# Reordering the opening of a convolution and feed-forward kernel: when the filter is turned, when two output rows are multiplied, and which PSUM tiles they use

## The chip, the cores and the metric

The kernel runs on one core of a Trainium2 chip. The metric is the device time of one execution in microseconds. A core has TensorE (PE for matmuls, PEld for the loading of their weights), VectorE (DVE), ScalarE (ACT), GpSimd (POOL) and SyncE (SP), each with its own queue of instructions that it works off in order. Matrix results are written to PSUM, from which VectorE and ScalarE copy them to SBUF. DMA transfers are issued from queues too, here mostly from SP and POOL.

## The reference

The input is x, 2048 tokens of 576 channels in bfloat16. Two layers of the same form follow each other, with the same weights:

```
x = x + A(layernorm(x))        # A: q * (causal convolution of kv along the tokens + kv * D)
x = x + B(layernorm(x))        # B: (gelu(x Wg) * (x Wu)) Wd, hidden width 4608
```

with, in A,

```
k_shift[t] = sum over j in 0..3 of shift_k[:, 3 - j] * k[t - j]
kv = k_shift * v
y  = irfft(rfft(kv padded) * rfft(ssm_k padded))[:2048] + kv * ssm_D
A  = q * y
```

The long convolution is along the tokens, one filter of 2048 taps for each of the 576 channels. The layer norms have no weights.

## The kernel before

**Blocks.** The tokens are cut into four blocks of 512, the feed-forward part into units of 512 tokens, and within a block a token t = 4q + i belongs to tile i (0 to 3), with q over 128 partitions. The convolution is done in blocks: each block of kv and each block of the filter is transformed by matmuls with tables of cosines and sines (`W`, `Wx`), the spectra are multiplied on VectorE, and the inverse transform is again a set of matmuls that sum up in PSUM. A spectrum has four parts kt of real and imaginary rows; the output has four tiles Y0 to Y3 (`straight(mt, kts)` issues, for output tile mt and each kt in kts, the products of two parts with two halves of 288 columns: four matmuls for each kt).

**The whole.** After an opening of some 38 us, written out by hand in `begin`, the feed-forward matmuls of the first unit begin (`half_gu`, line 1604), and from there to the end a planner (`Pace`, `fill`) lays the convolution of later blocks and all VectorE and ScalarE work between long runs of gate/up (line 1684) and down matmuls (line 1718). The planner works when the program is built, on its own estimates of time; the order it makes is fixed.

**The opening, in order of TensorE's work.** (1) Matmuls on constants fill the time until the first data come. (2) Small matmuls spread the short filter `shift_k` and the vector `ssm_D` over partitions. (3) The first block of k is turned (`L932`), four 128-column blocks minus the rest of the channels: 384 channels go by TensorE, 192 by VectorE (`wx`). (4) The first 512 taps of the filter, loaded as channels by taps in `hn[0]` (four blocks of 128 channels and one of 64, `nd` = 4), are turned by `turn_h(0)` (line 956) into two PSUM tiles, one for tiles i = 0 and 1, the other for 2 and 3, and ScalarE copies them to `hT0` (line 961). Before, POOL adds `ssm_D` to the filter's tap 0 (line 917), which lies in i = 0; `turn_h` therefore takes i in the order 2, 3, 1, 0. (5) `shift_taps` (line 817) convolves k with its four taps: 14 matmuls for the first two channel blocks, 7 for the third; VectorE multiplies them with v (line 977). (6) The transforms of filter and kv alternate (`even`, `odd` at line 227, `kfwd` at line 218). An `even` result is copied by ScalarE (line 990) before `odd` adds to the same PSUM tile; `apart` on VectorE (line 232) makes the two other spectrum parts from the two. `kacc(kt)` multiplies kv and filter spectra on VectorE (lines 358, 360, 361) and `put` writes spectra to DRAM from POOL's queue. (7) `turn_h(1)` turns the filter's second 512 taps. (8) `straight` makes Y0 and Y2, then Y1 and Y3 (line 414).

**The relay to the first feed-forward matmul.** For tiles 0 and 2: `head.gate` on VectorE multiplies with the normalized x and adds (lines 1493, 1496), `mean` and `sq` give mean and sum of squares (VectorE 1502, ScalarE 1219), `std` the root (ScalarE 1513), `norm` the normalized rows with their first 64 columns copied behind them (VectorE 1436, 1437, 1439), `turn` nine transposes on TensorE (line 1458), and `copy` brings them to `xnT` (line 1465) in two pieces of five and four column blocks. `keep_y` copies an output tile from PSUM to SBUF on ScalarE (line 420). Tiles 1 and 3 pass their gates a little later. `head.idle(6)` issues six transposes of a constant. A one-element Gelu (`warm`) makes ScalarE load the Gelu table.

**PSUM.** The pool `psp` (`new`, `new_t`, tag "pr") has three tiles of two banks, `cpsp` (`small`, `small_t`, tag "cps") has one. A tile that is asked for gets the space of one that is no longer needed, and its first matmul waits until the last reader is done. In the old order Y0 and Y2 lie in `psp`, Y1 and Y3 one after the other in the single tile of `cpsp`, and both pieces of a `head.turn` in one tile of `psp`.

**Queues around the change.** SP's queue holds the loads in the order k, filter rows 512 to 575, filter rows 0 to 511, v, x, the forward tables, the second filter block, the inverse tables (line 877), then three pairs of gate/up weights and, after the opening's scratch memory is free, three loads of down weights (line 1183). A load reuses one of a few semaphores and waits for the load that used it before. POOL's queue holds, mixed, small vector steps (the means of `act_sum` and `row_sum` at line 1211, the roots at 1226 and 1227), a rearrangement of `shift_k` that goes through DRAM (`skT`, lines 971, 973, 1048), and DMA issues; it also has a limited number of semaphores to reuse.

Of the kernel before, what the change touches and what calls it, by code (L numbers as in the profile page):

```python
# [22 lines left out]
P = 128  # L23
# [3 lines left out]
RT = BS // P  # L27
# [58 lines left out]
class Conv:  # L86
# [743 lines left out]
    def begin(self, head, tables):  # L830

        tc, nc, D, KS = self.tc, self.nc, self.D, self.KS
        nd = D // P
        width = lambda db: min(P, D - db * P)
        with ExitStack() as es:
# [12 lines left out]
            hn = [tmp.tile([P, nd + 1, BS], BF16, name=f"hn{b}") for b in range(2)]  # L848
            hT0 = tmp.tile([P, RT, D], BF16, name="hT0")
# [6 lines left out]

            def load_h(b):
                cols = slice(b * BS, (b + 1) * BS)
                nc.sync.dma_start(out=hn[b][0:D - nd * P, nd, :], in_=self.hk[nd * P:D, cols])
                nc.sync.dma_start(out=hn[b][:, 0:nd, :], in_=self.hk[0:nd * P, cols].rearrange("(b p) t -> p b t", p=P))  # L860

            nc.vector.memset(full, 1.0)
            nc.vector.memset(ones[:], 1.0)
# [26 lines left out]
            ps = new()  # L890
# [11 lines left out]
            ps = new()  # L902
# [10 lines left out]
            nc.scalar.copy(out=dcol[:, 0:nd], in_=ps[:, 1, at:at + nd])  # L913
            nc.scalar.copy(out=dcol[0:D - nd * P, nd:nd + 1], in_=ps[0:D - nd * P, 1, at + nd:at + nd + 1])
            busy(idle, 4)
            for lo, hi, w in ((nd, nd + 1, D - nd * P), (0, nd, P)):
                nc.gpsimd.tensor_tensor(out=hn[0][0:w, lo:hi, 0], in0=hn[0][0:w, lo:hi, 0], in1=dcol[0:w, lo:hi], op=ALU.add)

            k, v = self.kt_[0], self.vt_[0]
# [5 lines left out]
            DBS = [(0, 1), (2,)]  # L925
            pts = []
            for n, dbs in enumerate(DBS):
                pt = new_t() if n else small_t()
# [18 lines left out]
                tt(out=wx[0][:], in0=wx[0][:], in1=wx[1][:], op=ALU.add)  # L947
            tt(out=v[:, :, rest], in0=wx[0][:], in1=v[:, :, rest], op=ALU.mult)

            def turn_h(b, pt):  # L950

                hv = hn[b][:].rearrange("p b (q i) -> p b i q", i=RT)
                for i in (2, 3, 1, 0):
                    for db in range(nd + 1):
                        w = width(db)
                        nc.tensor.transpose(pt[i // 2][:, i % 2, db * P:db * P + w], hv[0:w, db, i, :], self.ident[0:w, 0:w])  # L956
                return pt

            def copy_h(hT, pt):
                for g in (1, 0):  # L960
                    nc.scalar.copy(out=hT[:, 2 * g:2 * g + 2, :], in_=pt[g][:, :, 0:D])
            copy_h(hT0, turn_h(0, (new_t(), new_t())))
            out = []
            for n, dbs in enumerate(DBS):
                o = (new() if n else small())[:].rearrange("p e (i c) -> p e i c", i=RT)
                for e, db in enumerate(dbs):
                    self.shift_taps(k, kT, dg, P, db, o[:, e])
                out.append(o)
            head.act_sum(3)
            for j in range(KS):  # L970
                nc.gpsimd.tensor_copy(out=self.skc[0:1, j, :], in_=sk1[:, :, j])
# [47 lines left out]
            def straight(mt, kts, first=False, last=False, parts=(0, 1)):  # L1019

                terms = []
                for kt in kts:
                    for part in parts:
                        if mt % 2 == 0:
                            s, minus = part, mt == 2 and kt % 2 == 1
                        elif kt % 2 == 0:
                            s, minus = part, kt == 2
                        else:
                            s, minus = 1 - part, ((mt == 1) == (part == 1)) != (kt == 3)
                        w = Wn[:, mt // 2, :] if minus and (mt, s) in ((1, 1), (3, 0)) else self.inv_w(mt, s, minus)  # L1030
                        terms.append((w, A[(part, kt)]))
                self.inverse(0, mt, terms, Y[mt], first, last)
# [47 lines left out]
            head.act_sq(1)  # L1080
            head.act_sq(3)
            head.gate(0, Y[0])
# [20 lines left out]
            nc.scalar.activation(out=warm[:], in_=head.zero, func=ACT.Gelu_apprx_tanh)  # L1103
# [705 lines left out]
```

## Time and profile before

| | us |
|---|---|
| median of 3 runs | 913.95 |
| the three runs | 914.36, 912.22, 913.95 |
| profiled execution | 912.26 |
| its span, first to last instruction | 910.4 |
| TensorE busy in the span | 904.5 |
| VectorE, ScalarE, POOL busy | 575.9, 331.6, 158.8 |
| first gate/up stream begins (line 1604) | 37.95 |

The profiled execution's time is longer than its span by 1.9 us, which lie around the instructions. A row of the timeline has start and length in microseconds from the span's start, the engine, the line of the kernel, the operation, output <- input by their names in the program with their sizes, and how many instructions the row joins; a bracket gives the engine's idle time before the first of them and what ended it. The start of the next row of an engine, rather than the end of the last, tells TensorE's pace, since its matmuls overlap. A row of a stage table has the stage's length, then busy time and count for PE, PEld, DVE, ACT and POOL, the granted clock, the DMA share and GB/s. Lines are those of the kernel before; in the changed kernel they move by up to 6.

### The profile page before, as it was taken

How to read it: one execution, taken by the hardware profiler on the slowest of the kernel's cores; microseconds unless marked ns; L12 is line 12 of the kernel's file. 1: busy time of each engine (PE TensorE's matmuls, PEld its weight loads, DVE VectorE, ACT ScalarE, POOL GpSimd, SP SyncE). 2: the span in 40 equal slices, each digit the busy share in tenths (PEclk: the TensorE clock that was granted, in tenths of full speed). 3: DMA queues.
4: the chain of work that ended last, by engine and by line, in shares of the span. 5: the costliest groups of instructions: out<-in, count | busy, mean ns of one | idle time of the engine just before them, and what ended most of it. 6: DMA issues, size and time to landing. Idle time of an engine off the chain costs nothing.

```text
span 910.4 us, 19239 instructions
## 1 busy us (share of the span) xinstructions
PE 904.5 (99%) x8173; PEld 526.6 (58%) x8173; DVE 575.9 (63%) x977; ACT 331.6 (36%) x621; POOL 158.8 (17%) x337
## 2 busy tenths in 40 slices
PE   9999999999999999999999999999999999999998
PEld 6786646556465465564655655646646546556555
DVE  7889986689889885797898855442332335333332
ACT  6765445523323255453124133551121224321211
POOL 3413405120113031420104002320000003100000
PEclk9999999999999999999999999999999999999999
DMA  9999998858519519785925801971620721977620
GB/s 250 351 217 282 238 253 131 208 157 170 183 53 249 123 16 168 211 154 114 268 65 131 181 2 38 170 159 26 132 78 4 154 80 27 170 171 178 135 64 27
DMA packets 129530, 131.73 MB, mean 145 GB/s; under 512 B 43682, under 2 KB 121251, under 8 KB 129444
## 3 DMA queue, kind: packets, MB, share of 16 engines
q1 hardware_dynamic: 119232, 93.47, 49.5%
q0 software_dynamic: 10208, 37.02, 13.0%
q8 instruction: 64, 1.05, 0.5%
q14 instruction: 22, 0.18, 0.1%
q10 hardware_dynamic: 4, 0.01, 0.0%
HBM read 108.35 MB, written 11.80 MB: 132 GB/s over the span
## 4 chain that ended last, share of the span: by engine, by line
PE 99%; ACT 0%; DMA 0%; DVE 0%; issue 0%; ACTq 0%; DVEq 0%
PE gu L1684 59%; PE dn L1718 31%; PE gu L1604 3%; PE cps L281 1%; PE ps L414 1%; PE cps L414 1%; PE ps L281 0%; PE ps L218 0%; PE cps L218 0%; PE ps L227 0%; PE pt L956 0%; DMA dvec<-in_A_ssm_D_dram 0%; PE xps L1458 0%; PE cps L817 0%; PE cpt L956 0%; PE cps L887 0%
## 5 line engine op out<-in xcount | busy, mean ns | idle before, releaser
L1684 PE MATMUL gu<-xnT,wgu 64*128 64x512 bf16 x4968 | 540.7, 376 | 0.0
L1684 PEld LDWEIGHTS <-wgu 64*128 64x128 bf16 x4968 | 239.7, 94 | 294.4 <-issue 5.7
L1693 ACT ACTIVATE ga<-gu 128x512 f32<-128x512 f32 x258 | 153.9, 597 | 450.9 <-PE gu L1684 442.5
L1694 DVE TENSOR_TENSOR hT<-ga,gu 128x512 bf16<-128x512 f32 x258 | 177.0, 686 | 200.7 <-ACT ga L1693 199.1
L1718 PE MATMUL dn<-wd,hT 128*128 128x288 bf16 x2304 | 292.3, 286 | 0.0
L1718 PEld LDWEIGHTS <-hT 128*128 128x128 bf16 x2304 | 223.5, 98 | 65.6 <-issue 9.5
L1754 DVE TENSOR_TENSOR x_c<-x_c,dn 128x576 f32<-128x576 f32 x64 | 48.2, 752 | 57.2 <-PE dn L1718 56.9
L1211 POOL TENSOR_SCALAR nm<-s 128x1 f32<-128x1 f32 x60 | 21.2, 354 | 271.6 <-DVE x_c L1749 210.8
L1219 ACT ACTIVATE junk<-x_c,nm 128x576 bf16<-128x576 f32 x48 | 36.8, 768 | 26.5 <-POOL nm L1211 25.9
L1227 POOL TENSOR_TENSOR rstd<-ve,neghalf_t 128x1 f32<-128x1 f32 x62 | 40.2, 648 | 5.2
L554 POOL DMA_DIRECT2D hr<-Hd x32 | 17.4, 544 | 118.3 <-DVE prod L360 117.3
L1226 POOL TENSOR_SCALAR ve<-ss 128x1 f32<-128x1 f32 x62 | 22.3, 360 | 54.4 <-ACT junk L1219 54.3
L1283 ACT ACTIVATE xn<-x_c,nb,rstd 128x576 bf16<-128x576 f32 (+1 forms) x48 | 28.6, 644 | 5.9 <-POOL nb L1231 5.7
L284 ACT COPY eo<-cps 128x576 f32<-128x576 f32 x31 | 19.9, 641 | 27.9 <-PE cps L281 24.4
L1740 DVE TENSOR_TENSOR ob<-x_c,dn 128x576 bf16<-128x576 f32 x15 | 11.3, 753 | 29.0 <-PE dn L1718 25.7
L1583 ACT ACTIVATE ga<-gu 128x512 bf16<-128x512 f32 x26 | 15.5, 597 | 31.8 <-PE gu L1684 24.9
L1604 PE MATMUL gu<-xnT,wgu 64*128 64x256 bf16 x432 | 24.8, 269 | 0.5 <-ACT xnT L1465 0.3
L1604 PEld LDWEIGHTS <-wgu 64*128 64x128 bf16 x432 | 21.2, 94 | 3.6 <-issue 1.1
L361 DVE TENSOR_TENSOR prod<-prod 128x576 bf16<-128x576 bf16 x48 | 22.0, 458 | 1.7
L429 POOL DMA_DIRECT2D out_dram<-ob x12 | 6.8, 562 | 91.8 <-issue 47.0
L244 DVE SCALAR_TENSOR_TENSOR eo<-eo 128x576 f32<-128x576 f32 x22 | 16.3, 752 | 5.8 <-ACT eo L284 5.8
L1261 DVE SCALAR_TENSOR_TENSOR x_c<-g_t,rstd,x_c 128x576 f32<-128x576 f32 x16 | 13.0, 815 | 8.6 <-POOL rstd L1227 8.6
(166 smaller groups left out, 589.9 us busy)
## 6 DMA issues: line engine op xcount, KB each, us to landing
wgu<-in_B_w_gate_dram SPq DMA_DIRECT2D x45, 576.0 KB, 6.5
wd<-in_B_w_down_dram SPq DMA_DIRECT2D x30, 864.0 KB, 8.3
wgu<-in_B_w_up_dram SPq DMA_DIRECT2D x45, 512.0 KB, 8.0
hr<-Hd POOLq DMA_DIRECT2D x32, 288.0 KB, 5.7
kr<-Kd POOLq DMA_DIRECT2D x24, 288.0 KB, 6.0
Kd<-kc POOLq DMA_DIRECT2D x12, 288.0 KB, 6.5
k<-in_A_k_dram POOLq DMA_DIRECT2D x3, 1008.0 KB, 12.4
wgu<-in_B_w_up_dram SPq DMA_DIRECT2D x45, 64.0 KB, 7.7
```

The source lines that it names most:

```text
L361: nc.vector.tensor_tensor(out=dst, in0=pr[:, 0, :], in1=pr[:, 1, :], op=ALU.subtract if part == 0 else ALU.add)
L1211: nc.gpsimd.tensor_scalar(out=v["nm"][:], in0=v["s"][:], scalar1=-1.0 / D, scalar2=None, op0=ALU.mult)
L1219: nc.scalar.activation(out=junk[:], in_=get_x(), func=ACT.Square, bias=v["nm"][:, 0:1], accum_out=v["ss"][:])
L1226: nc.gpsimd.tensor_scalar(out=ve[:], in0=v["ss"][:], scalar1=1.0 / D, scalar2=EPS, op0=ALU.mult, op1=ALU.add)
L1227: nc.gpsimd.tensor_tensor(out=v["rstd"][:], in0=ve[:], in1=neghalf_t[:, 0:1], op=ALU.pow)
L1283: nc.scalar.activation(out=xn[:, lo:hi], in_=x_c[c][:, j, 0:hi - lo], func=ACT.Identity, scale=v["rstd"][:, 0:1], bias=v["nb"][:, 0:1])
L1604: nc.tensor.matmul(pair[:, s, e * 256:(e + 1) * 256], lhsT=w[r0:r0 + HK, k, gi * P:(gi + 1) * P], rhs=xnT[r0:r0 + HK, blk_of[k], tok], sta ...
L1684: nc.tensor.matmul(pair[:, s, :], lhsT=w[r0:r0 + HK, k, gi * P:(gi + 1) * P], rhs=xnT[r0:r0 + HK, b, :], start=(k == 0), stop=(k == NKC - 1))
L1693: nc.scalar.activation(out=ga[:], in_=pair[:, 0, :], func=ACT.Gelu_apprx_tanh)
L1694: nc.vector.tensor_tensor(out=hT[:, fi, :], in0=ga[:], in1=pair[:, 1, :], op=ALU.mult)
L1718: nc.tensor.matmul(part[h][:, h, 0:HW], lhsT=hT[:, fi, at * P:(at + 1) * P], rhs=wd[2 * wb + fi // WT][:, fi % WT, h * HW:(h + 1) * HW], s ...
L1754: nc.vector.tensor_tensor(out=xh, in0=xh, in1=acc[:, :, 0:HW], op=ALU.add)
```

## The change

All of it lies in `begin`.

1. The filter loads change places (the 512 rows first, then the 64), and so do POOL's two additions of `ssm_D`.
2. `turn_h` takes a list of channel blocks and goes through i in order. For the first filter block the four blocks of 128 channels are turned and copied (two copies of 2 x 512 elements), then the first 14 `shift_taps` matmuls are issued, then the four 64-row turns and two copies of 2 x 64, then the last 7 taps. For the second filter block all 128-row turns come first and then the four 64-row ones; the `cps` tile is turned first, the copies stay as they were.
3. Of Y2's matmuls, those of kt = 0 alone (four) are issued ahead of Y0's last four, instead of those of kt = 0 and 2 (eight).
4. Y3 moves to a tile of `psp`. The six idle transposes go. `keep_y` of Y2 moves ahead, in front of tile 2's square, and that of Y1 behind tile 2's root; Y3's last four matmuls move ahead of tile 2's turn.
5. Tile 2's turn writes its first five blocks to a tile of `psp` and its last four to the one of `cpsp`. The one-element Gelu moves behind tile 2's copy.

The instructions after the opening, and their order on every engine, are the same in both kernels.

```
-                nc.sync.dma_start(out=hn[b][0:D - nd * P, nd, :], in_=self.hk[nd * P:D, cols])
                 nc.sync.dma_start(out=hn[b][:, 0:nd, :], in_=self.hk[0:nd * P, cols].rearrange("(b p) t -> p b t", p=P))
+                nc.sync.dma_start(out=hn[b][0:D - nd * P, nd, :], in_=self.hk[nd * P:D, cols])
...
-            for lo, hi, w in ((nd, nd + 1, D - nd * P), (0, nd, P)):
+            for lo, hi, w in ((0, nd, P), (nd, nd + 1, D - nd * P)):
...
-            def turn_h(b, pt):
+            def turn_h(b, pt, dbs):
                 hv = hn[b][:].rearrange("p b (q i) -> p b i q", i=RT)
-                for i in (2, 3, 1, 0):
-                    for db in range(nd + 1):
+                for i in range(RT):
+                    for db in dbs:
...
-            copy_h(hT0, turn_h(0, (new_t(), new_t())))
-            out = []
-            for n, dbs in enumerate(DBS):
-                o = (new() if n else small())[:].rearrange("p e (i c) -> p e i c", i=RT)
+            def taps_of(dbs, ps):
+                o = ps[:].rearrange("p e (i c) -> p e i c", i=RT)
                 for e, db in enumerate(dbs):
                     self.shift_taps(k, kT, dg, P, db, o[:, e])
-                out.append(o)
+                return o
+            pt, out = (new_t(), new_t()), []
+            turn_h(0, pt, range(nd))
+            copy_h(hT0, pt, slice(0, nd * P))
+            out.append(taps_of(DBS[0], small()))
+            turn_h(0, pt, (nd,))
+            copy_h(hT0, pt, slice(nd * P, D))
+            out.append(taps_of(DBS[1], new()))
...
-            copy_h(self.hT1, turn_h(1, (small_t(), new_t())))
+            pt = small_t(), new_t()
+            for dbs in (range(nd), (nd,)):
+                turn_h(1, pt, dbs)
+            copy_h(self.hT1, pt, slice(0, D), (1, 0))
...
             straight(0, (0, 2, 1), True)
-            straight(2, (0, 2), True)
+            straight(2, (0,), True)
             kacc(3)
             straight(0, (3,), last=True)
-            straight(2, (1, 3), last=True)
+            straight(2, (2, 1, 3), last=True)
...
-            self.keep_y(0, 1, Y[1])
-            head.idle(6)
-            Y[3] = small()
-            straight(3, (0, 2), True)
             head.gate(2, Y[2])
             head.mean(2)
+            self.keep_y(0, 2, Y[2])
+            Y[3] = new()
+            straight(3, (0, 2), True)
             head.sq(2)
             head.std(2)
             head.norm(0)
             head.turn(0)
             self.apart0(A, 0, 0)
-            straight(3, (1,))
+            straight(3, (1, 3), last=True)
+            self.keep_y(0, 1, Y[1])
             head.norm(2)
+            head.copy(0, nc.vector.tensor_copy)
+            head.turn(2, small_t())
+            head.copy(2, nc.scalar.copy, nc.vector.tensor_copy)
             nc.scalar.activation(out=warm[:], in_=head.zero, func=ACT.Gelu_apprx_tanh)
-            head.copy(0, nc.vector.tensor_copy)
-            head.turn(2)
-            straight(3, (3,), last=True)
-            head.copy(2, nc.scalar.copy, nc.vector.tensor_copy)
             self.keep_y(0, 3, Y[3])
-            self.keep_y(0, 2, Y[2])
```

More of the change, by code (lines that the diff above doesn't have):

```diff
@@ L948, in begin, with copy_h @@
             tt(out=v[:, :, rest], in0=wx[0][:], in1=v[:, :, rest], op=ALU.mult)
-            def turn_h(b, pt):
+            def turn_h(b, pt, dbs):
                 hv = hn[b][:].rearrange("p b (q i) -> p b i q", i=RT)
-                for i in (2, 3, 1, 0):
-                    for db in range(nd + 1):
+                for i in range(RT):
+                    for db in dbs:
                         w = width(db)
                         nc.tensor.transpose(pt[i // 2][:, i % 2, db * P:db * P + w], hv[0:w, db, i, :], self.ident[0:w, 0:w])
[L957 to L961, printed above, removed]
-            copy_h(hT0, turn_h(0, (new_t(), new_t())))
-            out = []
-            for n, dbs in enumerate(DBS):
-                o = (new() if n else small())[:].rearrange("p e (i c) -> p e i c", i=RT)
+            def copy_h(hT, pt, cols, order=(0, 1)):
+                for g in order:
+                    nc.scalar.copy(out=hT[:, 2 * g:2 * g + 2, cols], in_=pt[g][:, :, cols])
+            def taps_of(dbs, ps):
+                o = ps[:].rearrange("p e (i c) -> p e i c", i=RT)
                 for e, db in enumerate(dbs):
                     self.shift_taps(k, kT, dg, P, db, o[:, e])
-                out.append(o)
+                return o
[6 more added lines that the diff above has]
+            out.append(taps_of(DBS[1], new()))
             head.act_sum(3)
```

2 lines of the change are left out of this document (1 added, 1 removed).

## The prediction

> **What bounds the kernel now.** I read the page's busy shares, then stages by window, then the opening's timeline engine by engine (columns there: start, length, engine, line, operation, and in brackets the idle time before and what ended it).
>
> ```profile
> PE 904.5 (99%) x8173; PEld 526.6 (58%) x8173; DVE 575.9 (63%) x977; ACT 331.6 (36%) x621; POOL 158.8 (17%) x337
> ```
>
> ```profile
> 7.00:38.00 31.00, 29.56 (x254) 22.35 (x254) 26.44 (x53) 25.57 (x47) 14.55 (x29) 1.00 1.08 304
> 38.00:910.40 872.40, 869.29 (x7880) 500.33 (x7879) 545.87 (x905) 302.85 (x567) 143.10 (x301) 1.00 0.61 138
> ```
>
> From 38 us on TensorE (the column after the length) has no idle time worth a name: 869.29 of 872.40. What the opening gains before its first gate/up matmul therefore reaches the end, and what it loses too. The instruction order after that point is the same in both kernels.
>
> In the opening the page hides the bound: PE is "busy", but for two stretches another engine sets the pace.
>
> ```profile
> 5.69 0.56 DVE L942 TENSOR_TENSOR wx<-k,sx 128x768 bf16<-128x768 bf16 x1 [0.44 <-ACT sx L912]
> 5.84 0.45 POOL L917 TENSOR_TENSOR hn<-hn,dcol 64x1 bf16<-64x1 bf16 x1 [4.55 <-ACT dcol L914]
> 6.00 1.06 PE L932 MATMUL cpt<-ident,k 128*128 128x128 bf16 x8
> 6.86 0.63 PE L932 MATMUL pt<-ident,k 128*128 128x128 bf16 x4
> 7.09 0.55 DVE L946 TENSOR_TENSOR wx<-kx,sx 128x768 bf16<-128x768 bf16 x1
> 7.10 1.01 ACT L937 COPY kT<-cpt 128x1024 bf16<-128x1024 bf16 x1 [0.15 <-PE cpt L932]
> 7.36 2.70 PE L956 MATMUL pt<-ident,hn 128*128 128x128 bf16 x20
> 7.38 0.32 POOL L917 TENSOR_TENSOR hn<-hn,dcol 128x4 bf16<-128x4 bf16 x1 [1.09 <-DMA hn<-in_A_ssm_k_dram]
> 8.01 0.59 ACT L937 COPY kT<-pt 128x512 bf16<-128x512 bf16 x1
> 10.00 1.92 PE L817 MATMUL cps<-dg,kT 128*128 128x512 bf16 x14
> 11.12 0.69 ACT L1204 ACTIVATE junk<-x_b 128x576 bf16<-128x576 bf16 x1
> 11.75 1.03 PE L817 MATMUL ps<-dg,kT 128*128 128x512 bf16 x7
> 12.62 1.14 PE L227 MATMUL ps<-hT,W 128*128 128x288 bf16 x8
> 15.12 0.72 POOL L973 DMA_DIRECT2D skT<-skc  x1 [0.31 <-POOL skc L971]
> ```
>
> ```profile
> 15.36 1.42 DVE L232 SCALAR_TENSOR_TENSOR h<-eo,ps 128x576 bf16<-128x576 f32 x2 [0.93 <-ACT h L995]
> ...
> 28.29 0.46 DVE L361 TENSOR_TENSOR yb<-prod 128x576 bf16<-128x576 bf16 x1
> 30.03 0.81 DVE L1493 SCALAR_TENSOR_TENSOR x_c<-x_b,nm,ps 128x576 f32<-128x576 bf16 x1 [1.29 <-PE ps L414]
> ```
>
> VectorE runs from 15.36 to 28.75 without a recorded wait: its last product (kacc(3)) cannot come earlier unless 15.36 does, and that waits for TensorE's first transform through ScalarE. From 30.03 a relay runs: gate, mean, square, root, norm, turn, copy, first gate/up matmul at 37.95.
>
> **First turns and taps.** Turns are paced by TensorE's rate: eight from 6.00 to 6.86, 0.107 us each; late ones take 0.056 (below: nine from 34.91 to 35.41). The 20 before last 7.36 to 10.00. Afterwards the first turn needs the D-added row, so it waits for POOL's 128x4 add. The large load is issued first now; its landing (about 7.36 before) can move by the small load's share only, a tenth of its bytes, to 7.05 at best. POOL's two L917 adds both ended 0.05 to 0.06 after a VectorE tensor_tensor (5.69+0.56 against 5.84+0.45; 7.09+0.55 against 7.38+0.32), so I take the same end, 7.70, and the first turn at 7.75; the other bound is no wait, 7.28. Sixteen turns of 0.107 bring the taps to 9.5; 14 taps last 1.75 (10.00 to 11.75), to 11.25. The four 64-row turns: in the second tile ten turns last 0.97 (24.83 to 25.80, below), eight of them 0.45, so a lone 64-row turn costs 0.26, mostly the switch of row count before and after. Four together: 0.26+3x0.056=0.43, bounded by 4x0.26=1.04. Taps of the last block, 0.87, end at 12.55 instead of 12.62: **gain 0.07**, between -0.54 and +0.34. Their four copies become two of 1024 and two of 128 elements (1.01 each, and by the slope from 0.59 to 1.01 about 0.28, at most 0.59); they end about 12.3, hidden while the taps run to 12.55, and act_sum (0.69) behind them ends 13.0, before ScalarE's next copy can start, after the transform's first four matmuls (0.123 each, below; 12.55+0.49+0.2=13.2).
>
> [...]
>
> **Second turns, and Y2 behind Y0.**
>
> ```profile
> 24.83 1.04 PE L956 MATMUL pt<-ident,hn 128*128 128x128 bf16 x10
> 25.80 1.07 PE L956 MATMUL cpt<-ident,hn 128*128 128x128 bf16 x10
> 26.80 4.09 PE L414 MATMUL ps<-yb,W 128*128 128x288 bf16 x32
> 30.73 0.90 PE L414 MATMUL cps<-yb,W 128*128 128x288 bf16 x6
> ```
>
> The 20 turns shrink from 1.97 to 16x0.056+0.43=1.33: PE reaches Y0 at 26.09. A product matmul takes 3.93/32=0.123. Twelve of Y0 and four of Y2 end 28.06, two more 28.30; the last pair needs kacc(3), 28.75-0.07=28.68. So Y0's last starts 28.85 instead of 29.63 (26.80+23x0.123), and the gate starts at 29.25 instead of 30.03: 0.78, of it **0.71 new**. PE idles 0.4 there; with eight of Y2 ahead it would be there at 28.5 and lose nothing, so the moved four are worth nothing if the turns shrink, and up to 0.49 if they don't. The turns' first half now waits for kc's copy out of the single cps tile; that copy follows the same matmuls that PE has just left, and is done about 0.1 before PE comes; each 0.1 late would cost nothing either until the 0.4 idle is used up.
>
> **The relay's end.**
>
> ```profile
> 32.80 0.82 DVE L1496 SCALAR_TENSOR_TENSOR x_c<-x_c,rstd,x_b 128x576 f32<-128x576 f32 x1
> 33.25 0.63 ACT L420 ACTIVATE y<-cps 128x576 bf16<-128x576 f32 x1
> 33.94 0.65 PE L414 MATMUL cps<-yb,W 128*128 128x288 bf16 x4 [0.74 <-ACT y L420]
> 34.91 0.67 PE L1458 MATMUL xps<-ident,xn 128*128 128x128 bf16 x9
> 35.19 1.28 ACT L1103 ACT_TABLE_LOAD   x1
> 35.41 0.65 PE L414 MATMUL cps<-yb,W 128*128 128x288 bf16 x4
> 36.02 0.18 DVE L1439 COPY xn<-xn 128x64 bf16<-128x64 bf16 x1
> 36.04 0.68 PE L1458 MATMUL xps<-ident,xn 128*128 128x128 bf16 x9
> 36.11 0.81 DVE L1465 COPY xnT<-xps 128x640 bf16<-128x640 bf16 x2
> 36.75 0.69 ACT L1465 COPY xnT<-xps 128x640 bf16<-128x640 bf16 x1
> 37.35 2.83 SPq L1183 DMA_DIRECT2D wd<-in_B_w_down_dram  x3
> 37.48 0.42 DVE L1465 COPY xnT<-xps 128x512 bf16<-128x512 bf16 x1 [0.55 <-ACT xnT L1465]
> 37.95 5.96 PE L1604 MATMUL gu<-xnT,wgu 64*128 64x256 bf16 x106 [0.17 <-DVE xnT L1465]
> ```
>
> Y3 leaves the single cps tile, so the 0.74 wait on Y1's copy goes, and the six idle matmuls (6x0.056) that lay in it; keep_y(2) takes that copy's place (0.63) before the second square. Norm 2 ends at 36.20-0.78=35.42. PE must not be late: 16 of Y1 and 8 of Y3 end 33.4, turn 0 starts at 33.8 with its norm, eight of Y3 end 35.28, norm 2's rows come at 35.20: level. Its fifth turn waits for the 128x64 copy (35.47), done 35.69; ScalarE's copy 35.73 to 36.42; VectorE, after turn 0's copies (35.33+0.81=36.14), copies the other four blocks from their own tile without the 0.55 wait for ScalarE: 36.1 to 36.52. The stream starts at 36.57 instead of 37.95: **another 0.60**, down to 0 if that wait returns in another form.
>
> Given back: the Gelu table load and its warm-up move behind ScalarE's copy and hold Y3's copy to 36.42+1.28+0.2+0.63=38.5, which tile 3's gate reads. VectorE, after tile 1's gate (two passes of 0.81 and 0.82 from 36.52, with small steps between), would want it at 38.3. If tiles 1 and 3 come 0.2 late to their turns, PE may wait that long: I charge 0.1, between 0 and 0.2. SP's three wd loads wait for that warm-up: 37.9 instead of 37.35; the gate/up matmuls cover them, the first down matmul starting at 64.83-1.38. On SP the inverse twiddles (L877) and the first wgu load behind them now wait for the large hn load instead of the small one:
>
> ```profile
> 64.83 0.42 PE L1718 MATMUL dn<-wd,hT 128*128 128x288 bf16 x2
> ```
>
> these are first read at 26.1 and 36.5, so a slip of a microsecond or two costs nothing.
>
> **Sum.** 0.07+0.71+0.60-0.1=1.3 us. The profiled execution took 912.26 for a span of 910.4; the sum gives 910.95. That execution is quick: the runs took 914.36, 912.22 and 913.95 (median 913.95, mean 913.5), a spread of 2.1 that no row explains. From the mean, 912.2. I forecast the middle, **911.6**. Changes within 0.3% (2.7 us) are about what a measurement of this kernel can't tell from none.
>
> **Rivals.**
> 1. The relay's end pays nothing: 0.60 lost to a new wait (PE late at turn 2, ScalarE's y2 copy late, 0.63, ahead of the square). For it: both meet within 0.1 us. Gain 0.7: 912.2. Chance 0.17.
> 2. Full rate comes late, and it ends slower. The spacing fell from 0.107 to 0.056 near 9.5, inside the turns. The halt before the first turn could delay that. Each us longer costs 0.48; from 2.7 us later (12.2) the gain is gone, and 3.5 later, the length from 6.00 to 9.5, gives 1.7 lost: 913.3, where the kernel before stands at 911.6+1.3=912.9. Against: the halt is 0.4 at most. Chance 0.1.
> 3. POOL's queue slips. act_sum ends 1.1 later, so skT (15.12) leaves later, and with it the POOL DMAs ahead of tile 2's rstd.
>
> ```profile
> 28.35 0.54 POOL L424 DMA_DIRECT2D Hd<-h  x1 [2.44 <-DVE prod L360]
> 29.20 0.56 POOL L1227 TENSOR_TENSOR rstd<-ve,neghalf_t 128x1 f32<-128x1 f32 x1
> ```
>
> The 2.44 wait absorbs 1.1; rstd (29.76) is needed at 32.80-0.78=32.0. From 3.3 late on each us costs one: at 5 late the 1.7 lost give 913.3. Chance 0.05.
> 4. The change does more: the add doesn't wait (0.34) and nothing is given back: 0.34+0.71+0.60=1.65, 911.2. Chance 0.13.
>
> The forecast keeps 0.55. [...]
>
> Range 909.8 to 914.0: the upper gain from the quickest run, less run scatter, to the lost gain from the slower runs. Against 913.95, faster by over 0.3% means under 911.2: a third of the forecast's and half of rival 4's weight and a little of rival 1, 0.31. Slower by over 0.3% needs two of the losses together: 0.07.
>
> **What would show it.** First L956 at 7.3 to 7.8, 16 turns 1.7 long; first L227 near 12.5; VectorE's gate L1499 near 29.3 with PE waiting for DVE yb before Y0's last pair; no ACT y wait before Y3; the gate/up stream at 36.6, VectorE's last xnT copy not waiting for ScalarE. Wrong if the 64-row turns cost 0.26 each in a row, if PE still takes 0.107 per turn or more past 10, or if the stage after 38 shows new PE gaps.

## The result and the profile after

The changed kernel takes 910.68 us (median of ten runs, 909.91 to 911.10), the kernel before 912.65 (ten runs, 911.75 to 915.46): the ratio is 0.9971, with a 95% interval of 0.9961 to 0.9982, that is 1.6 to 3.6 us less. The forecast was 911.6, its range 909.8 to 914.0. The profiled executions took 912.26 before and 910.61 after, their spans 910.4 and 908.8.

First the page's busy shares of the changed kernel, and its two stages by window (columns as before):

```profile
PE 903.0 (99%) x8167; PEld 526.0 (58%) x8167; DVE 575.7 (63%) x977; ACT 331.6 (36%) x623; POOL 157.7 (17%) x337
```

```profile
7.00:38.00 31.00, 29.63 (x278) 23.49 (x278) 27.93 (x55) 26.08 (x49) 13.94 (x28) 1.00 1.08 301
38.00:908.80 870.80, 867.61 (x7852) 498.53 (x7846) 544.07 (x901) 302.35 (x567) 142.53 (x301) 1.00 0.61 139
```

Behind 38 us TensorE idles 3.19 us, 3.11 before: nothing new there, and the 1.60 by which that stretch is shorter was won ahead of it. So the opening has to be read. The timeline of the changed kernel, first turns and taps:

```profile
5.85 0.36 POOL L917 TENSOR_TENSOR hn<-hn,dcol 128x4 bf16<-128x4 bf16 x1 [4.55 <-DMA hn<-in_A_ssm_k_dram]
6.43 0.19 POOL L917 TENSOR_TENSOR hn<-hn,dcol 64x1 bf16<-64x1 bf16 x1 [0.23 <-DMA hn<-in_A_ssm_k_dram]
7.17 1.91 PE L956 MATMUL pt<-ident,hn 128*128 128x128 bf16 x16
8.88 2.24 PE L817 MATMUL cps<-dg,kT 128*128 128x512 bf16 x14
11.05 0.32 PE L956 MATMUL pt<-ident,hn 64*128 64x64 bf16 x4
11.30 1.05 PE L817 MATMUL ps<-dg,kT 128*128 128x512 bf16 x7
12.19 1.14 PE L227 MATMUL ps<-hT,W 128*128 128x288 bf16 x8
14.93 1.42 DVE L232 SCALAR_TENSOR_TENSOR h<-eo,ps 128x576 bf16<-128x576 f32 x2 [1.19 <-ACT h L1000]
```

POOL's add to the large part is done at 6.21, where the prediction had 7.70. The first turn (7.17, 7.36 before) waits for nothing; of these 0.19, 0.08 is the wait for the load that TensorE had before, and 0.11 is chance: the D vector that TensorE spreads at L909 came at 4.25 here and at 4.36 in the profile before. Then the sixteen turns take 1.71 (7.17 to 8.88), and the first transform comes at 12.19: 0.43 earlier than the 12.62 before. VectorE's first sum follows 0.43 earlier too (14.93, 15.36 before). The same view, second turns and first gate:

```profile
24.40 0.61 PE L956 MATMUL cpt<-ident,hn 128*128 128x128 bf16 x8
25.48 0.23 PE L956 MATMUL pt<-ident,hn 64*128 64x64 bf16 x2
25.64 2.38 PE L414 MATMUL ps<-yb,W 128*128 128x288 bf16 x18
28.36 1.88 PE L414 MATMUL ps<-yb,W 128*128 128x288 bf16 x14 [0.34 <-DVE yb L361]
28.88 0.81 DVE L1499 SCALAR_TENSOR_TENSOR x_c<-x_b,nm,ps 128x576 f32<-128x576 bf16 x1 [0.58 <-PE ps L414]
```

The second turns take 1.24 (24.40 to 25.64) instead of 1.97. TensorE has eighteen matmuls done and waits 0.34 for VectorE's last product, as forecast. The gate is at 28.88, 1.15 earlier than before, 0.72 of it new. The relay's end, again in the timeline:

```profile
33.41 0.68 PE L1464 MATMUL xps<-ident,xn 128*128 128x128 bf16 x9 [0.24 <-DVE xn L1443]
35.39 0.69 ACT L1471 COPY xnT<-xps 128x640 bf16<-128x640 bf16 x1 [0.67 <-PE xps L1464]
35.69 0.41 DVE L1471 COPY xnT<-cpt 128x512 bf16<-128x512 bf16 x1
36.09 1.28 ACT L1114 ACT_TABLE_LOAD   x1
36.13 4.11 PE L1610 MATMUL gu<-xnT,wgu 64*128 64x256 bf16 x72 [0.56 <-DVE xnT L1471]
37.50 0.63 ACT L420 ACTIVATE y<-ps 128x576 bf16<-128x576 f32 x1
38.16 0.82 DVE L1499 SCALAR_TENSOR_TENSOR x_c<-x_b,nm,y 128x576 f32<-128x576 bf16 x1 [0.22 <-ACT y L420]
```

(The Gelu table load is line 1103 before and 1114 here, since it moved.) The two last copies run side by side (35.39 to 36.08 and 35.69 to 36.10). Before, the first two gate/up matmuls had run at 37.49 and the third at 37.95; now the third starts at 36.24, 0.11 behind the first. From the gate to the third the relay took 7.92 (30.03 to 37.95) and takes 7.36 (28.88 to 36.24): 0.56 less. With it the stream is 1.71 earlier, and the span 1.66 shorter (910.41 and 908.75).

**The times hold something that no single profile does.** The ten runs of the kernel before fall into two groups: six from 911.75 to 912.72, four from 913.95 to 915.46. All ten of the changed kernel lie within 1.2 us. The mean of the short six, 912.24, is 1.69 above the mean of the ten changed runs, 910.55, about what the two spans show. Which part of the change took the second group away was the first question for the experiments.

### The profile page after: what moved, and what is told of

Same layout as the page of the kernel before. It is cut to its first block, busy times and chain, and to the rows that moved or that the text cites. A ratio compares the mean times of both kernels' runs of the same rounds, so it can differ in the third digit from the quotient of the medians.

```text
span 908.8 us, 19231 instructions
## 1 busy us (share of the span) xinstructions
PE 903.0 (99%) x8167; PEld 526.0 (58%) x8167; DVE 575.7 (63%) x977; ACT 331.6 (36%) x623; POOL 157.7 (17%) x337
## 4 chain that ended last, share of the span: by engine, by line
PE 97%; DVE 2%; ACT 0%; issue 0%; DVEq 0%; ACTq 0%
PE gu L1690 59%; PE dn L1724 31%; PE gu L1610 3%; PE cps L281 1%; PE ps L414 1%; PE cps L414 0%; PE ps L281 0%; DVE yb L361 0%; PE cps L887 0%; DVE h L232 0%; DVE prod L360 0%; DVE prod L358 0%; PE cps L817 0%; PE pt L956 0%; DVE x_c L1502 0%; DVE x_c L1499 0%
```

## Experiments

Twelve sets of runs in three groups; those of a group ran on one chip, with runs of the kernel before beside them. Each quoted text is what was expected before the run. In the diffs some lines are shortened. "First transform" is the first L227 matmul. "Doubling" is where the spacing of TensorE's consecutive matmul starts in the trace falls from 0.83 ns per column to 0.43, read to about 0.2 us.

| kernel | runs, median (range) us | first turn | doubling | first transform | gate | third gate/up | span |
|---|---|---|---|---|---|---|---|
| before (profiled) | | 7.36 | 9.5 | 12.62 | 30.03 | 37.95 | 910.41 |
| changed (profiled) | 10, 910.68 (909.91-911.10) | 7.17 | 9.5 | 12.19 | 28.88 | 36.24 | 908.75 |
| u1_first | 12, 913.05 (910.77-914.32) | 8.30 | 14.0 | 15.18 | 31.89 | 39.25 | 911.75 |
| u2_turns | 6, 910.72 (910.10-911.55) | 7.20 | 7.7 | 11.44 | 28.37 | 35.72 | 908.24 |
| u3_y2 | 5, 910.14 (909.83-911.34) | 7.14 | 9.7 | 12.25 | 28.96 | 36.31 | 908.88 |
| u4_relay | 6, 910.66 (910.38-911.59) | 7.11 | 10.5 | 12.64 | 29.36 | 37.28 | 909.74 |
| b_load | 11, 912.20 (911.75-914.24) | 7.20 | 8.6 | 12.21 | 29.63 | 37.56 | 910.01 |
| w5_pool | 10, 912.86 (911.27-913.91) | 8.43 | 13.9 | 14.85 | 31.55 | 38.89 | 911.41 |
| w8_pool | 9, 914.32 (914.13-915.36) | 10.16 | 16.0 | 16.76 | 33.46 | 40.81 | 913.32 |
| f0_nofill | 7, 909.76 (909.49-910.92) | 6.89 | 10.3 | 12.52 | 29.21 | 36.56 | 909.07 |
| after_again | 11, 909.82 (909.70-910.93) | 7.13 | 8.6 | 11.69 | 28.39 | 35.74 | 908.38 |
| a16_4 | 11, 910.19 (909.60-911.41) | 7.09 | 8.1 | 11.45 | 28.15 | 35.50 | 908.01 |
| u7_onetile | 10, 910.84 (910.38-912.62) | 7.23 | 8.4 | 11.65 | 28.36 | 36.28 | 908.74 |
| v2_best | 7, 909.73 (909.39-909.98) | 6.89 | 8.3 | 11.44 | 28.13 | 35.48 | 907.98 |

The doubling moves by almost 3 us between executions in which TensorE isn't halted before the first turn (7.7 to 10.5), and the first transform with it. A turn takes 0.107 us before it and 0.056 behind it, so a doubling that comes 1 us later costs 0.48 us; 2.8 us of it are 1.3 us of time, about the 1.2 over which the ten runs of the changed kernel lie. So the parts are compared by distances behind it (transform to gate, gate to third gate/up matmul), which it doesn't touch.

### First group: one part put back at a time

**The first tile's part put back (u1_first)**

```
-                dma hn[b][:, 0:nd, :]; dma hn[b][0:D - nd * P, nd, :]
+                dma hn[b][0:D - nd * P, nd, :]; dma hn[b][:, 0:nd, :]
...
-            turn_h(0, pt, range(nd)); copy; taps_of(DBS[0], small())
-            turn_h(0, pt, (nd,)); copy; taps_of(DBS[1], new())
+            turn_h(0, pt, range(nd + 1), (2, 3, 1, 0)); copy by halves
+            taps_of(DBS[0], small()); taps_of(DBS[1], new())
```

(POOL's two adds swapped back as well.)

> The changed kernel with the first tile's part alone put back: the small load of hn first, POOL's small add first, twenty turns row by row, their copies by halves, and all taps behind them. Theory: VectorE's products run without a wait from the first transform to the gate, so what the first transform loses reaches the end. First transform matmul at 12.6 us (12.19 in the changed kernel, 12.62 in the one before), second tile's turns at 24.8 (24.40), first gate at 29.3 (28.88), span 0.43 us longer, 909.2. Rival: TensorE's 0.34 us idle before Y0's last pair takes the loss up; gate at 28.9, span 908.8. On the scatter of the kernel before (six of ten runs at 911.8 to 912.7, four at 914.0 to 915.5): if the late landing of the hn load makes it, this kernel's runs scatter by 2 us and those of the other three put-backs don't.

Both groups of times are back: five runs from 910.77 to 911.59, seven from 913.00 to 914.32; the kernel before had 14 of 19 at 913.5 and above beside them. The other three put-backs have no run above 911.59. So the second group comes with the first tile's part, as expected. The execution profiled here is one of the long ones (913.60), and its timeline shows what the profile of the kernel before, a short one, could not:

```profile
8.32 0.45 POOL L917 TENSOR_TENSOR hn<-hn,dcol 128x4 bf16<-128x4 bf16 x1 [2.15 <-DMA hn<-in_A_ssm_k_dram]
8.30 2.95 PE L956 MATMUL pt<-ident,hn 128*128 128x128 bf16 x20 [0.93 <-DMA hn<-in_A_ssm_k_dram]
11.19 3.29 PE L817 MATMUL cps<-dg,kT 128*128 128x512 bf16 x14
15.18 1.14 PE L227 MATMUL ps<-hT,W 128*128 128x288 bf16 x8
```

The large load lands at 8.3 instead of 7.3. Fourteen of its sixteen completion marks are there by 6.85, the other two come at 8.13 and 8.26; of the next load, v, fourteen are there by 8.35 and two come at 9.55 and 9.70. What is late is a small part of a load. TensorE halts 0.93 for it, and then keeps half its rate to 14.0: the fourteen taps start at 11.19 and the next seven only at 14.31, 3.12 later, where 1.75 do at full rate. The first transform comes 2.56 later than in the kernel before. The sum agrees: 0.94 of halt, and half rate for the rest of the 4.5 us by which the doubling is later, 3.56x0.48=1.71, together 2.65.

From the first transform to the gate it takes 16.71, the changed kernel 16.69: whatever the first transform loses or wins reaches the gate in full. The rival, that TensorE's 0.34 idle takes it up, falls. (The 12.6 and 909.2 of the expectation are for an execution without the halt; none of this kernel was profiled.)

**The second tile's turns put back (u2_turns)**

```
-            for dbs in (range(nd), (nd,)):
-                turn_h(1, pt, dbs)
+            turn_h(1, pt, range(nd + 1), (2, 3, 1, 0))
```

> The changed kernel with the second tile's twenty turns row by row again, the 64-row ones between the others. Theory (prediction's step 2): the turns take 1.97 us instead of 1.24, Y0 starts at 26.37 instead of 25.64, eighteen matmuls of 0.123 later is 28.58, where VectorE's last product is there at 28.31: Y0's last pair is 0.25 late, the gate at 29.15 instead of 28.88, the span 909.1. Rival: the whole 0.73 is paid, gate at 29.6, span 909.5. Other rival: nothing is paid, 908.8, if the eighteen matmuls don't fill the time.

The absolute times are earlier than expected because the rate doubled at 7.7 here. The distance is what tells:

```profile
23.65 1.04 PE L956 MATMUL pt<-ident,hn 128*128 128x128 bf16 x10
25.62 3.60 PE L414 MATMUL ps<-yb,W 128*128 128x288 bf16 x28
28.37 0.81 DVE L1498 SCALAR_TENSOR_TENSOR x_c<-x_b,nm,ps 128x576 f32<-128x576 bf16 x1 [0.79 <-PE ps L414]
```

The turns take 1.97 again, Y0's matmuls run without a gap, and from the first transform the gate comes after 16.93, against 16.69: 0.24 lost, as the theory had it (0.25), not 0.73.

**Eight of Y2 ahead again (u3_y2)**

```
-            straight(2, (0,), True)
+            straight(2, (0, 2), True)
...
-            straight(2, (2, 1, 3), last=True)
+            straight(2, (1, 3), last=True)
```

> The changed kernel with eight of Y2's matmuls ahead of Y0's last again, instead of four. Theory (prediction: the moved four are worth nothing if the turns shrink): 22 matmuls of 0.123 from 25.64 end at 28.34, just when the last product comes; gate at 28.9 to 29.0 and span 908.8 to 908.9, TensorE's idle 0.34 gone from that place without a gain. Rival: the four pay their full length, 0.49: gate at 29.37, span 909.3.

```profile
25.69 4.13 PE L414 MATMUL ps<-yb,W 128*128 128x288 bf16 x32
28.96 0.81 DVE L1499 SCALAR_TENSOR_TENSOR x_c<-x_b,nm,ps 128x576 f32<-128x576 bf16 x1 [0.58 <-PE ps L414]
```

TensorE's gap is gone from that place and the gate comes 16.71 after the first transform: 0.02. The moved matmuls are worth nothing while the turns are short. With both parts old (the kernel before) the distance is 17.41, so with long turns they are worth 17.41-16.93=0.48.

**The relay's end put back (u4_relay)**: the order and tiles of the kernel before from Y1's copy to Y3's.

```
+            self.keep_y(0, 1, Y[1])
+            head.idle(6)
+            Y[3] = small()
...
-            head.turn(2, small_t())
+            head.turn(2)
```

> The changed kernel with the relay's end put back: Y3 in the single cps tile behind Y1's copy, six idle matmuls, Gelu's table ahead of the copies, the second tile's turn in one PSUM tile. Gate at 28.88 as before it. Theory, by the third gate/up matmul (two of them ran ahead of the last copy in the kernel before, 0.22 us of work that the prediction counted as gained): it comes 7.92 after the gate, 36.80 instead of 36.35, and the span is 0.45 longer, 909.2. The prediction's own size: 0.60, 909.4. Rival 1 of the prediction (the relay's end pays nothing): 908.8.

```profile
29.36 0.81 DVE L1501 SCALAR_TENSOR_TENSOR x_c<-x_b,nm,ps 128x576 f32<-128x576 bf16 x1 [0.58 <-PE ps L414]
36.80 0.42 DVE L1473 COPY xnT<-xps 128x512 bf16<-128x512 bf16 x1 [0.55 <-ACT xnT L1473]
37.28 1.47 PE L1612 MATMUL gu<-xnT,wgu 64*128 64x256 bf16 x23 [0.17 <-DVE xnT L1473]
```

From the gate 7.92, exactly as before, and with it the 0.55 wait. The expectation's correction to 0.45 was a slip: it took two gate/up matmuls for 0.22 us where they are 0.11 apart in all, and put the changed kernel's third at 36.35 instead of 36.24. The loss is 0.56, near the prediction's 0.60. Rival 1, nothing paid, falls.

### Second group: where the long runs come from

**The load order alone, in the kernel before (b_load)**

```
-                dma hn[b][0:D - nd * P, nd, :]; dma hn[b][:, 0:nd, :]
+                dma hn[b][:, 0:nd, :]; dma hn[b][0:D - nd * P, nd, :]
```

(and POOL's two adds likewise)

> The kernel before with two pairs of lines swapped and nothing else: the large load of hn is issued before the small one, and POOL adds to the large part first. Theory: half and more of the runs of the kernel before are 2 us longer because the load that comes second in the queue lands late (8.28 us in the profile of the put-back of the first part, 7.3 in that of the kernel before), TensorE halts 0.93 us for it, and its rate then doubles only at 14.0 us instead of 9.5. With the large load first the first turn is at 7.1 to 7.2 with no halt over 0.3; all runs lie between 911 and 913, median 912.2, while the kernel before beside it keeps runs of 914 and more. Rival: the long runs come from another piece of the first part (order of the 64-row turns, the copies); then this kernel scatters like the one before, median 913.5 or more.

```profile
5.96 0.28 POOL L917 TENSOR_TENSOR hn<-hn,dcol 128x4 bf16<-128x4 bf16 x1 [4.67 <-DMA hn<-in_A_ssm_k_dram]
7.20 2.46 PE L956 MATMUL pt<-ident,hn 128*128 128x128 bf16 x20
9.59 1.92 PE L817 MATMUL cps<-dg,kT 128*128 128x512 bf16 x14
```

Partly missed. The profiled execution has the first turn at 7.20 and no halt over 0.1, and eight runs lie between 911.75 and 912.34, but three are at 913.98 to 914.24 (the kernel before beside it: 9 of 28 at 913.5 and more). In this kernel the fifth turn, a 64-row one, needs the small load, which is now second in the queue. It had landed at 6.7 in this execution, at 7.0 to 7.4 in those of u2_turns, u3_y2, u4_relay and a16_4. That a landing as late as u1_first's 8.3 makes the three long runs is argued, not shown: no long run of this kernel was profiled, so for these three the expectation's rival isn't excluded.

In the executions without a halt the load order is worth nothing by itself: span 910.01 with the doubling at 8.6, 910.41 with it at 9.5, 0.9x0.48=0.43. Against after_again, whose rate doubled at 8.6 too, the first transform comes 0.52 later (12.21, 11.69): that is, to about 0.1, what the 64-row turns between the others cost. So what the first part gains without a halt, 0.43, comes mostly from the grouping of these turns and not from the order of the loads.

**A halt without a late load (w5_pool, w8_pool)**

```
+            for n in range(5):      # 8 in w8_pool
+                nc.gpsimd.tensor_tensor(out=jk[:], in0=(jk if n else dcol)[:, 0:nd], in1=dcol[:, 0:nd], op=ALU.add)
             for lo, hi, w in ((0, nd, P), (nd, nd + 1, D - nd * P)):
```

> The changed kernel with five more small additions on POOL (128x4, into a tile that nothing reads) between the D values and the add to hn: the loads land as in the changed kernel, but the first turn is held back, by an estimate from the 0.36 us of the 128x4 add and its shorter neighbours by 0.3 to 0.9 us. Theory that a short halt costs itself and no more: doubling of the rate stays between 7.7 and 10.5 us and the time is 910.9 to 911.4. Theory that a halt of this size already costs the early doubling: it comes between 11.5 and 14.5, time 912.5 to 914.

> The same with eight additions: the first turn held back by 1.0 to 2.0 us. Theory (the halt puts off the full rate): without a halt the rate doubled 3.5 to 6.2 us after TensorE's last gap, at 4.25; counted from the end of the halt that is 11.9 to 15; the time is 912.8 to 914.8. Rival (the long runs of the kernel before are a state of the DMA queues, and the rate follows the time since the start): doubling stays between 7.7 and 10.5, the halt costs itself at most, 911.4 to 912.2.

The added POOL work took 0.48 to 0.52 us an instruction (1.90 for four, 3.67 for seven), so both halts are longer than estimated (the first turn is 1.26 and 2.99 later than in the changed kernel). w5_pool, then w8_pool:

```profile
8.43 1.89 PE L959 MATMUL pt<-ident,hn 128*128 128x128 bf16 x16 [1.02 <-POOL hn L920]
10.12 3.62 PE L817 MATMUL cps<-dg,kT 128*128 128x512 bf16 x14
14.85 1.14 PE L227 MATMUL ps<-hT,W 128*128 128x288 bf16 x8
```

```profile
10.16 1.90 PE L959 MATMUL pt<-ident,hn 128*128 128x128 bf16 x16 [2.79 <-POOL hn L920]
11.85 3.62 PE L817 MATMUL cps<-dg,kT 128*128 128x512 bf16 x14
16.76 1.14 PE L227 MATMUL ps<-hT,W 128*128 128x288 bf16 x8
```

No load is waited for (POOL's add follows its additions at 8.17 and 9.90 without a recorded wait) and POOL causes the halt, yet the rate doubles at 13.9 and 16.0: 5.5 and 5.8 after the halt's end, as in u1_first (5.7). The first transform is 2.66 and 4.57 later than in the changed kernel. So a halt of about 1 us cost some 2.6 us, made by a load (0.93 cost 2.56 in u1_first) or by POOL (1.02 cost 2.66 in w5_pool), against an execution whose rate doubles at 9.5. The rival's claim that the rate follows the time since the start falls. Its other half, that the state of the queues makes the long runs, isn't touched: it was a late load that halted u1_first.

Nine of w5_pool's ten runs lie from 912.60 to 913.91, as the second theory has it; one, 911.27, is as short as the first theory has it, and no profile shows why. For w8_pool the doubling (16.0, expected 11.9 to 15) and four of the nine runs (914.98 to 915.36, expected up to 914.8) are later than forecast, because its halt is longer than forecast. How short a halt is forgiven isn't known: both came out above 1 us.

Without a halt the doubling lay 3.5 to 6.3 us after TensorE's one-column matmuls near 4.2 (L909) in the executions with fillers (7.7 to 10.5), so the 5.5, 5.7 and 5.8 after a halt lie within what is seen without one. What sets the moment within that stretch of 2.8 us no run shows.

**Without the four fillers (f0_nofill)**

```
-            busy(idle, 4)
```

> The changed kernel without the four filler matmuls (128x256, 0.85 us at the slow rate) that TensorE runs ahead of the key's shift and turns. Theory: TensorE has its work then without a gap, the first turn comes at 6.4 to 6.6, when POOL's add is done (6.2 to 6.5), the doubling lies in the same stretch as without, and 0.85 us less of slow work is worth 0.4 us: median 910.2. Rival: the fillers are what counts as work for the clock, the doubling comes 1 us or more later and eats it, 910.6 to 911.5. Other rival: the add to hn now holds TensorE for 0.3 us or more and the full rate is put off as in the put-back of the first part, 912.5 or more.

```profile
4.82 0.40 PE L909 MATMUL ps<-ones,dvec 1*128 1x1 bf16 x5 [0.49 <-DMA dvec<-in_A_ssm_D_dram]
```

The median is 909.76, six of seven runs are at 909.96 or below, and the profiled one is the seventh, 910.92. The first turn came at 6.89, not 6.5: the D vector landed at 4.8 in this execution instead of 4.2 to 4.3 and held TensorE back 0.49 (the same in v2_best; nothing ahead of that place differs in these programs, so why stays open). The doubling, 10.3, is inside the stretch seen with the fillers, so it isn't shown that the fillers bear on it. v2_best below has the comparison on one chip.

### Third group: the changed kernel beside its variants

**The changed kernel again (after_again)**

> The changed kernel as it is, beside the next three on one chip. If its gain in the median comes from halts that it can no longer have, all its runs lie between 909.8 and 911.3 again and none at 912 or above, whatever the kernel before shows here. If the ten runs seen so far were luck, some of these lie above 912.

Eleven runs from 909.70 to 910.93, a little lower than expected and none long. Their mean, 910.16, is 1.76 below that of the 21 short runs of the kernel before beside them (911.92). Over all four sets of runs 35 of 86 of the kernel before are at 913.5 or above, and none of 21 of the changed kernel is above 911.10.

**The 64-row turns right behind the others (a16_4)**

```
             turn_h(0, pt, range(nd))
-            copy_h(hT0, pt, slice(0, nd * P))
-            out.append(taps_of(DBS[0], small()))
             turn_h(0, pt, (nd,))
-            copy_h(hT0, pt, slice(nd * P, D))
+            copy_h(hT0, pt, slice(0, D))
+            out.append(taps_of(DBS[0], small()))
```

> The changed kernel with the first tile's four 64-row turns right behind the sixteen full ones, ahead of all taps, and their copies with the others. Theory: what counts is that no turn before 8.9 us needs the load that comes second in the queue (it landed between 6.3 and 8.3), and that the 64-row turns stand together; behind the two blocks' taps they gain nothing more. No halt over 0.3, runs between 909.8 and 911.3, first transform as late after the doubling as in the changed kernel. Rival: the taps are needed as cover, a third or so of the runs are at 912.5 and above, as three of eleven were with the load order alone.

```profile
7.09 1.80 PE L956 MATMUL pt<-ident,hn 128*128 128x128 bf16 x20
8.83 1.92 PE L817 MATMUL cps<-dg,kT 128*128 128x512 bf16 x14
11.45 1.14 PE L227 MATMUL ps<-hT,W 128*128 128x288 bf16 x8
```

The doubling is 0.46 earlier than in after_again and the first transform 0.24, which is half of it: nothing is left for the place of the four turns. The means, 910.28 and 910.16, don't tell them apart, and the runs lie from 909.60 to 911.41, just past both ends of what was expected. That the four stand together and behind the sixteen is enough; the taps as cover are not needed here.

**Tile 2's turn in one PSUM tile (u7_onetile)**

```
-            head.turn(2, small_t())
+            head.turn(2)
```

> The changed kernel with the second tile's turn (tile 2 of the relay) in one PSUM tile instead of two. Theory: VectorE's copy of the last four blocks waits for ScalarE's copy of the first five again, 0.35 to 0.55; from the first gate to the third gate/up matmul 7.36 becomes 7.7 to 7.9, the time 0.3 to 0.5 longer, 911.0. Rival: the copies no longer meet there and nothing is lost: 7.36, 910.6.

```profile
35.80 0.42 DVE L1471 COPY xnT<-xps 128x512 bf16<-128x512 bf16 x1 [0.56 <-ACT xnT L1471]
35.82 0.28 PE L1610 MATMUL gu<-xnT,wgu 64*128 64x256 bf16 x2 [0.78 <-ACT xnT L1471]
36.28 1.49 PE L1610 MATMUL gu<-xnT,wgu 64*128 64x256 bf16 x24 [0.17 <-DVE xnT L1471]
```

The wait is back with 0.56, and from the gate to the third gate/up matmul it takes 7.92: without the second PSUM tile nothing of the relay's gain is left. The second tile without the other moves was not run. The mean is 0.85 above after_again's beside it, 0.56 of which the trace accounts for. One run, 912.62, stands apart from the rest (911.43 and below) without an explanation.

**Without fillers, rows in the old order (v2_best)**

```
-            busy(idle, 4)
...
-            turn_h(0, pt, range(nd))
-            copy_h(hT0, pt, slice(0, nd * P))
+            turn_h(0, pt, range(nd), (2, 3, 1, 0))
+            copy_h(hT0, pt, slice(0, nd * P), (1, 0))
```

> The changed kernel without the four fillers and with the first tile's sixteen turns in the rows' old order (2, 3, 1, 0): the rows that POOL's add changes are turned last, so nothing waits for it. First turn at 6.3 to 6.5, no halt, 0.8 us less of slow work ahead of the doubling, worth 0.4 to 0.5: median 910.1 where the changed kernel beside it has 910.6. Rival: the large load itself (5.7 to 6.1) or the D values come late in some runs, and a halt of TensorE at 6.3 puts off the full rate: some runs at 912 and more. Other rival: nothing gained, since VectorE's own chain to the first transform sets the time.

The runs lie from 909.39 to 909.98 with median 909.73 and mean 909.70, where after_again has 909.82 and 910.16. The medians are 0.09 apart, the means 0.46: a little better at most. The first turn, 6.89, follows TensorE's own work without a halt; the D vector was late again.

## Why the prediction was right, and where it was wrong

The direction, the sizes of two of the three gains, and the time within the range were right. The likeliest case was not quite what came; its place is rival 4's, at 0.13. Part of the agreement in the absolute time is luck. The forecast put the kernel before at 912.9 by halving the way between a short run and a mean of three, and the median of ten is 912.65; in the other three sets it was 914.14, 912.41 and 912.12, as more or fewer of the runs were long.

**First turns and taps: wrong in its first term.** The step that failed is the landing of the large load, "7.05 at best", taken from the small load's share of the bytes. It was there at 5.70 in the changed kernel, and by 6.13 in every execution that issues it first. In the trace, the 16 completion marks of the load lie between 5.82 and 7.32 where it is issued second, with packets of the next load (4608 bytes, its own have 1024) between its own from 5.4 on, and between 5.30 and 5.70 where it is first. So POOL's add was done at 6.21, again 0.07 behind the VectorE tensor_tensor beside it (5.58 to 6.14), as the prediction had read the two before; only both were long past when TensorE came. The gain is 0.43, not 0.07, and above the 0.34 given as upper end. (No working of 0.34 is given; the bound without a wait, 7.28 for 7.75, makes it 0.54, less what the taps lose by running ahead of the doubling.) The fourteen taps did take longer than the 1.75 assumed: from 8.88 to the four turns at 11.05 it is 2.17, 0.10 of it the first half of the switch to 64 rows and the rest because they now begin ahead of the doubling. The sixteen turns are as forecast (1.71); the group of four adds 0.35 where 0.43 stood: it lies between two tap starts 0.51 apart (10.79 and 11.30) where 0.16 would do without it.

**Second turns, and Y2 behind Y0: right.** The turns take 1.24 (1.33 forecast), TensorE idles 0.34 (0.4), and the new gain at the gate is 0.72 (0.71). The two statements on the moved four hold as well: 0.02 with short turns, 0.48 (up to 0.49 forecast) with long ones. The time given for the first, TensorE "there at 28.5" with eight of Y2 ahead, is a slip: 22 matmuls from 26.09 end at 28.80, 0.12 behind the product's 28.68, so by its own sum about 0.1 would have been lost.

**The relay's end: right in size, and the cause is one of the two named.** 0.56 for 0.60. It is the copies' meeting in one PSUM tile: u7_onetile keeps the moves that take away Y3's 0.74 wait on Y1's copy and put the Gelu table behind, and loses everything, so these gave nothing without the second tile.

**Given back: 0.05 for 0.1.** The Y3 copy ran at 37.50 and tile 3's gate waited 0.22 for it, behind the stream. The stream is 1.71 earlier and the span 1.66 shorter; that this wait is what makes the 0.05 is not shown.

**Sum.** 0.43+0.72+0.56-0.05=1.66, against 1.3; the profiled executions differ by 1.65. That the terms add up to it is no proof, since all are read from these two traces; the put-backs are. It is rival 4's sum (0.34+0.71+0.60=1.65) with rival 4's reason, that the add doesn't hold the turn; that it agrees to the hundredth, with the terms up to 0.09 apart, is chance.

**Rival 2, on the other kernel.** "The halt before the first turn could delay" the full rate: the effect is real, as u1_first, w5_pool and w8_pool show (doubling at 14.0, 13.9 and 16.0 instead of 9.5), and costs what rival 2 feared, but the changed kernel doesn't have the halt. That the kernel before has it in its long runs (35 of 86) is concluded from u1_first, which shares its first part: no long run of the kernel before itself was profiled, and the three of b_load aren't explained. The prediction called the spread of its three runs one "that no row explains" and set the base between its own profile and their mean. The spread was the second half of the change's worth: about 1.7 against the short runs, and 2.2 to 2.4 more against the long ones, by the means of the four sets. From the quick profile alone the prediction's own sum gave 910.95, where 910.68 was measured. Rivals 1 and 3 didn't come. The relay's end paid. skT left 0.54 later (15.66, 15.12), POOL's wait of 2.44 shrank to 1.45, and rstd was there at 29.72, with the gate's second pass at 31.65.

That the spacing fell "inside the turns" stands on the profile before: TensorE ran nothing but turns from 6.00 on, and their spacing fell from 0.107 to 0.056 at 9.5, among them.

## What to carry to other kernels

Where the runs of a kernel fall into two groups and one profile exists, the profile is of one group: look for the wait that was nearly zero in it (here 0.08 us before the first turn) and ask what a late landing would set off. In a start that still ran at half rate a halt of about 1 us cost 2.6 (2.56 in u1_first, 2.66 in w5_pool), so work that depends on the last transfers belongs behind work that doesn't. A PSUM tile shared by two engines' copies serialised them for 0.56 us; the second tile took the wait away, and reordering without it brought nothing.

## What the runs showed of the hardware that was not expected

- The granted clock reads 1.00 in every microsecond from 6 to 15, also where TensorE runs at half rate. The same stretch of taps by window, in the kernel before and in u1_first (columns: window, length, TensorE's busy time and its instructions, clock, DMA share, GB/s):

```profile
11.00:12.00 1.00, 1.00 (x10) 1.00 1.09 323
```

```profile
11.00:12.00 1.00, 1.00 (x5) 1.00 1.08 350
```

  Ten taps a microsecond and five, with "1.00" busy and "1.00" granted in both: only the spacing of starts tells.
- Of two loads issued 0.5 to 0.6 us apart on one queue, the large one lands whole at 5.7 to 6.1 in each of the twelve executions that issue it first; the second, large or small, anywhere from 6.2 to 8.3.
- Small additions on POOL (128x4 in float32) took 0.48 to 0.52 us each in a chain in w5_pool and w8_pool. The add of 128x4 in bfloat16 took 0.21 us in one execution (a16_4) and 0.51 in another (v2_best), so the time of one doesn't tell that of five.
